# An attention and gated feed-forward kernel on one core: token chunks of 512, one per batch, in place of chunks of 384

## Chip, cores and metric

The kernel runs on one NeuronCore of a Trainium2 chip. The metric is device microseconds (us) of one execution of the whole program; the median of several runs is compared. Five engines work side by side, each through its own instructions in program order: TensorE (PE, matmuls; PEld is its weight load, which runs beside the matmuls), VectorE (DVE), ScalarE (ACT), GpSimd (POOL) and SyncE (SP, which here only issues DMA transfers).

## What is computed

Eight batches of 576 tokens, eight heads of 64. Heads 0 to 3 attend to a local window of 32 tokens, heads 4 to 7 to the tokens whose position has the same remainder by 32. The 4608 x 512 result goes through a feed-forward layer with a gate.

```python
batch, n_heads, seq, head_dim = (8, 8, 576, 64)
mask_local = (rel >= 0) & (rel < stride)            # stride = 32
mask_strided = (rel >= 0) & (pos[None, :] % stride == pos[:, None] % stride)
...
attn = attn / (np.sum(attn, axis=-1, keepdims=True) + 1e-09)
...
# n_tokens, d_model, d_ff = (4608, 512, 2048)
h = x @ w_in
sp = np.maximum(h, 0.0) + np.log1p(np.exp(-np.abs(h)))
g = h * erf(sp)
return (g @ w_out).astype(np.float32)
```

## The kernel before

**Feed-forward.** The tokens are cut into twelve chunks of `CH` = 384 (line 20), three for each pair of batches: the first lies in the even batch, the second takes the last 192 tokens of the even and the first 192 of the odd batch, the third lies in the odd batch. For each chunk and each of the sixteen 128-column slices f of the hidden layer, `ftile` (line 665) does one set of work. `mm1` (line 674, its matmul is line 678) makes h as 12 matmuls of 384 columns: every fp32 operand is held as a high and a low fp32r part (`xhi`, `xlo` and the pair of each weight), and three of the four products are taken for each of four slices of the model dimension. Then ten steps on ACT and DVE turn h into the gated g and split it: `n1` (ACT, reads the PSUM bank of h), `n2` (DVE), `n3`, `n4` (ACT), `n5`, `n6` (DVE), `n7`, `gate` (ACT), `prod` (DVE, writes the product back into the bank of h), `split_hi` (ACT, line 716) and `split_lo` (DVE, line 719). ACT's functions are recorded at line 686, DVE's three-operand steps at line 683. `mm2` (line 747, matmul at line 750) is nine matmuls of 512 columns, three for each of the three 128-token tiles, added up in three output banks `o0` to `o2` over the slices f. After the last f of a segment ACT copies each output bank to `ob` (`evac`, line 766) and SP stores it (line 769); later segments of the same chunk are added in DRAM by a DMA that POOL issues (line 772).

**Order of the first chunks.** While the weights come in, the first three chunks are worked in turns, four slices at a time: `SEGS` (line 84) has nine segments, (0,0,4), (1,0,4), (2,0,4), (0,4,8) and so on, the last three being slices 8 to 16. From chunk 3 on, a chunk runs through all sixteen slices. `weight` (line 610) loads each of 32 weight slices as 64-bit numbers and makes fp32 and then the pair of it: three bit operations and a subtraction on DVE, a cast on ACT (lines 628 to 649).

**Attention.** `heads` (line 324) does one unit of two heads, 4 units a batch, 32 in all: q, k and v are loaded by SP (lines 378 and 386), 80 or 48 small matmuls make scores (line 400), maximum, difference, exponential and sum follow on DVE and ACT, POOL divides (`norm`, line 498), PE transposes (line 507), ACT copies the result to a tile `pt` (line 513), 72 or 44 small matmuls make x (line 526), and ACT and DVE split x into `xhi` and `xlo` (lines 545 and 550). These two hold a ring of two batches of tokens. A unit of batch b writes its part of the ring after the chunks that read the batch two before it have been through `mm1`.

**What sets the order.** `Plan` (line 158) writes out one fixed order for each engine ahead of time, from keys (`FT`, `KW`, `KP`, `SLOT`) and a model of durations; the engines then run that order and wait on semaphores. `bufs` (line 301) gives the number of buffers of each kind: 3 banks for h, 2 buffers each for `a`, `b`, `ghi`, `glo`, `sm` and `pt`, and one bank each for `o0` to `o2`. Two more PSUM banks belong to attention. `TWO` (line 144) names the DVE steps that the plan keeps apart from POOL's work. Until the first feed-forward work PE fills gaps with matmuls on constants (`warm`, line 858).

```python
            terms = [(w, x, cc) for w, x in ((0, xhi), (1, xhi), (0, xlo)) for cc in range(NCC)]
            for i, (w, x, cc) in enumerate(terms):
                yield nc.tensor.matmul(
                    ph[:, :CH], win[4 * s + cc][:, w, fs], x[cc][:, c0 : c0 + CH], start=(i == 0), stop=(i == len(terms) - 1)
                )
```

Of the kernel before, what the change touches and what calls it, by code (L numbers as in the profile page):

```python
# [19 lines left out]
CH = 384  # L20
NCHUNK = NT // CH
# [8 lines left out]
SLOT = 4.6  # L30
BACKLOG = 1.1130116
FT = (31.6335, -135.614, 224.291, 52.3709, -149.741, 22.9733, 45.4447, 151.185, -55.3448, 2.76331, -71.5147, 15.0393)
KI = 6.0
KW = (
# [4 lines left out]
)  # L39
KP = (  # L40
    (10.1977, 20.0763, 41.7156, 4.63147, -42.1192, -1.63969, 44.6351),
    (-59.6923, -46.4572, 19.3027, 2.1291, -1.1102, -2.7047, 19.8359),
    (0.362135, -29.4861, 70.4804, -32.303, -26.5488, -31.8946, 13.368),
    (35.4136, 29.0365, 82.2259, 1.42982, 5.30056, -34.5623, 14.0121),
    (39.729, -4.01849, 28.501, 2.48999, 23.3488, 1.39481, -48.8561),
    (39.4267, -19.5662, -38.0465, 15.7041, 15.7802, 2.62076, 21.1909),
    (86.1182, 25.9137, 40.603, 35.2787, 19.0606, 47.8996, 48.8007),
    (66.293, 47.5794, 1.05774, -1.16663, 5.84633, 49.4365, 8.65975),
    (130.703, 144.013, 104.668, 48.8468, 193.869, 96.8577, 143.58),
    (64.6189, 239.715, 128.496, 148.929, 218.31, 111.72, 213.914),  # L50
    (83.8361, 207.928, 161.012, 201.508, 232.12, 168.377, 236.359),
    (122.833, 130.354, 229.613, 323.83, 280.389, 244.736, 254.984),
    (275.847, 231.102, 232.486, 247.903, 285.925, 244.698, 249.036),
    (249.04, 261.206, 282.841, 273.283, 271.781, 286.07, 316.395),
    (257.063, 302.313, 270.687, 300.842, 280.135, 302.865, -52.5488),
    (271.303, -41.686, 283.568, 283.624, 288.229, 313.902, -30.1178),
# [908 lines left out]
```

## Time and profile before

| | |
|---|---|
| three runs | 931.13, 931.49, 933.93 us; median 931.49 us |
| profiled execution, its own time | 933.05 us |
| its span, first to last instruction | 931.3 us |
| busy: PE, PEld | 909.7 us (98%), 809.6 us (87%) |
| busy: DVE, ACT, POOL | 686.7 us (74%), 653.4 us (70%), 60.9 us (7%) |
| mean granted TensorE clock | 0.993 of full |

A share of busy time is a mean over stages with different limits. The stages here are: until 43.7 us attention of the first batches and loads, without feed-forward work; until about 200 us feed-forward while weights are still being made; until about 733 us feed-forward with attention of later batches between; until 917.9 us feed-forward alone; then the end. A matmul's duration in a row holds its way through the array and overlaps the next one's, so what a matmul costs is read from the distance between starts.

### The profile page before, as it was taken

To read this page: it belongs to the slowest core of one execution; us is meant where nothing else is said; L and a number is where in the kernel's file an instruction comes from. 1 tells how busy PE (TensorE), PEld (TensorE's weight loads), DVE (VectorE), ACT (ScalarE), POOL (GpSimd) and SP (SyncE) were. 2 spreads that over 40 slices of the span, in tenths; PEclk is the share of its full clock that TensorE was granted. 3 is DMA by queue.
4 is the path that set the end of the run, shared out by engine and by line. 5 is a ranking of instruction groups with operands and counts; after the bars stand their busy time and mean duration, and the time that the engine had idled before them with its cause. 6 is when DMAs were issued, how large, how long until landed. Compare 5 with 4: busy or idle time off the path is not lost.

```text
span 931.3 us, 20134 instructions
## 1 busy us (share of the span) xinstructions
PE 909.7 (98%) x8166; PEld 809.6 (87%) x8169; DVE 686.7 (74%) x1352; ACT 653.4 (70%) x1476; POOL 60.9 (7%) x59
## 2 busy tenths in 40 slices
PE   5789999999999999999999999999999999999998
PEld 4678888898888889988888899998898899999997
DVE  5999999996757766669886876667876666666664
ACT  5687887887776767667666666766766766766765
POOL 2200012110101100001110100000100000000000
PEclk9799999999999999999999999999999999999999
DMA  9994124321313010013312300002300200000000
GB/s 336 391 362 154 62 57 73 61 34 48 78 58 86 30 64 35 27 57 105 99 56 92 124 17 1 34 1 73 135 1 30 70 1 1 34 1 0 34 1 35
DMA packets 23421, 68.86 MB, mean 74 GB/s; under 512 B 2592, under 2 KB 3232, under 8 KB 23328
## 3 DMA queue, kind: packets, MB, share of 16 engines
q1 hardware_dynamic: 20736, 62.86, 18.9%
q0 software_dynamic: 2592, 4.72, 3.6%
q8 instruction: 64, 1.05, 0.5%
q14 instruction: 29, 0.24, 0.1%
HBM read 53.41 MB, written 14.16 MB: 73 GB/s over the span
## 4 chain that ended last, share of the span: by engine, by line
PE 90%; DVE 4%; ACT 3%; issue 1%; DMA 1%; SPq 0%; POOL 0%; ACTq 0%; POOLq 0%
PE h L678 41%; PE o L750 40%; PE s L400 3%; PE x L526 3%; PE t L507 2%; PE s L526 1%; DMA qk<-qk_loc 1%; ACT b L686 1%; DVE a L683 1%; DVE b L683 1%; ACT a L686 1%; PE s L507 1%; DVE glo L719 1%; ACT sm L472 0%; DVE h L713 0%
## 5 line engine op out<-in xcount | busy, mean ns | idle before, releaser
L750 PE MATMUL o<-pair,ghi 128*128 128x512 f32 x1152 | 361.4, 395 | 0.2 <-ACT ghi L716 0.2
L678 PE MATMUL h<-xhi,pair 128*128 128x384 f32 x1536 | 302.4, 339 | 0.6 <-DVE glo L719 0.6
L678 PEld LDWEIGHTS h<-xhi,pair 128*128 128x128 f32 x1536 | 271.4, 188 | 16.5 <-DVE glo L719 2.6
L686 ACT ACTIVATE b<-b 128x384 f32<-128x384 f32 x384 | 200.4, 522 | 77.2 <-DVE b L683 73.8
L750 PEld LDWEIGHTS o<-pair,ghi 128*128 128x128 f32 x1152 | 209.8, 188 | 32.4 <-ACT ghi L716 0.7
L750 PE MATMUL o<-pair,glo 128*128 128x512 f32 x576 | 224.8, 390 | 0.0
L683 DVE SCALAR_TENSOR_TENSOR a<-h,a 128x384 f32<-128x384 f32 x192 | 106.3, 553 | 83.3 <-ACT a L686 82.8
L678 PE MATMUL h<-xlo,pair 128*128 128x384 f32 x768 | 164.4, 336 | 0.0
L686 ACT ACTIVATE a<-h 128x384 f32<-128x384 f32 x192 | 93.5, 487 | 100.9 <-PE h L678 100.2
L683 DVE SCALAR_TENSOR_TENSOR a<-a,h 128x384 f32<-128x384 f32 x192 | 105.5, 549 | 68.9 <-ACT b L686 68.9
L713 DVE TENSOR_TENSOR h<-b,h 128x384 f32<-128x384 f32 x192 | 107.0, 557 | 46.2 <-ACT b L686 45.8
L678 PEld LDWEIGHTS h<-xlo,pair 128*128 128x128 f32 x768 | 136.0, 188 | 0.0
L750 PEld LDWEIGHTS o<-pair,glo 128*128 128x128 f32 x576 | 108.1, 188 | 23.7 <-DVE glo L719 0.3
L686 ACT ACTIVATE a<-a 128x384 f32<-128x384 f32 x192 | 100.3, 523 | 26.6 <-DVE a L683 26.1
L719 DVE TENSOR_TENSOR glo<-h,ghi 128x384 fp32r<-128x384 f32 x192 | 105.7, 550 | 11.7 <-ACT ghi L716 10.2
L716 ACT CAST ghi<-h 128x384 fp32r<-128x384 f32 x192 | 90.5, 471 | 29.1 <-DVE h L713 15.1
L683 DVE SCALAR_TENSOR_TENSOR b<-b,a 128x384 f32<-128x384 f32 x192 | 108.7, 566 | 1.0
L686 ACT ACTIVATE b<-a 128x384 f32<-128x384 f32 x192 | 101.0, 526 | 4.4
L498 POOL TENSOR_TENSOR sm<-sm,r 128x768 f32<-128x768 f32 (+3 forms) x36 | 45.0, 1249 | 435.3 <-DVE r L491 330.9
L436 DVE TENSOR_REDUCE mx<-s 128x12 f32<-128x768 f32 (+3 forms) x37 | 28.8, 784 | 10.6 <-PE s L413 10.3
L766 ACT COPY ob<-o 128x512 f32<-128x512 f32 x54 | 31.0, 588 | 2.7 <-PE o L750 2.2
L526 PEld LDWEIGHTS x<-pt,v 64*64 64x64 f32 x1392 | 24.4, 135 | 6.9 <-issue 4.4
(49 smaller groups left out, 511.4 us busy)
## 6 DMA issues: line engine op xcount, KB each, us to landing
out<-ob SPq DMA_DIRECT2D x36, 256.0 KB, 2.0
v<-v_loc SPq DMA_DIRECT2D x13, 640.0 KB, 4.1
words<-w_in SPq DMA_DIRECT2D x16, 512.0 KB, 8.6
words<-w_out SPq DMA_DIRECT2D x16, 512.0 KB, 9.1
qk<-qk_loc SPq DMA_DIRECT2D x13, 592.0 KB, 3.8
qk<-qk_str SPq DMA_DIRECT2D x12, 608.0 KB, 3.8
v<-v_str SPq DMA_DIRECT2D x16, 384.0 KB, 3.3
out<-ob POOLq DMA_DIRECT2D x18, 256.0 KB, 4.6
```

The lines of the kernel that those rows point to most:

```text
L436: yield nc.vector.tensor_reduce(out=mx[:, parts[i], :units], in_=wide(of(s, i)), axis=mybir.AxisListType.X, op=ALU.max)
L498: yield (nc.gpsimd if pool_norm else nc.vector).tensor_tensor(out=d, in0=d, in1=spread(rc, i), op=ALU.mult)
L507: yield nc.tensor.transpose(bank(t, h)[:, 128 * w : 128 * w + 128], sm[:, h, c : c + 128], ident)
L526: yield nc.tensor.matmul(bank(px, m)[h * D : (h + 1) * D, a * n : (a + 1) * n], values(rows, (2 * a + h) * D), pt[rows, h, c : c + n], sta ...
L678: yield nc.tensor.matmul(ph[:, :CH], win[4 * s + cc][:, w, fs], x[cc][:, c0 : c0 + CH], start=(i == 0), stop=(i == len(terms) - 1))
L683: yield nc.vector.scalar_tensor_tensor(out=out, in0=in0, scalar=scalar, in1=in1, op0=op0, op1=op1)
L686: yield nc.scalar.activation(dst, src, func, bias=bias[i], scale=scale)
L713: yield nc.vector.tensor_tensor(out=ph[:, :CH], in0=bb.tile, in1=ph[:, :CH], op=ALU.mult)
L716: yield nc.scalar.copy(ghi.tile, ph[:, :CH])
L719: yield nc.vector.tensor_tensor(out=glo.tile, in0=ph[:, :CH], in1=ghi.tile.bitcast(F32), op=ALU.subtract)
L750: yield nc.tensor.matmul(po.tile, g[:, ts], wout[f][:, w], start=(f == first_f and i == 0), stop=(f == last_f and i == 2),)
L766: yield nc.scalar.copy(ob.tile, po.tile)
```

## The change

Chunks have 512 tokens: chunk b is the first 512 tokens of batch b. The last 64 tokens of each batch, in `xhi` and `xlo`, are written by SP to a tensor `rests` in DRAM as soon as a unit of attention has made them (64 transfers of 128 rows of 256 bytes); after batch 7 and after chunk 6 has been through its `mm1`, POOL issues eight loads that bring them back, and they make chunk 8. So there are nine chunks and 144 sets in place of twelve and 192. `mm1` has 12 matmuls of 512 columns, `mm2` 12 for four token tiles and four output banks `o0` to `o3`; h has two PSUM banks in place of three. A new step `keep` on ACT copies h from PSUM to an SBUF tile `hs` (three buffers); `n5`, `prod`, `split_hi` and `split_lo` then read `hs` and not the bank, and `prod` writes into `hs`. `n6`, `n7` and `gate` work in `a`, so that `b` is free after `n6`; `b` has one buffer. `SEGS` has six segments of the first two chunks. `pt` shares the buffer of `sm`. Chunk 8's rows are stored by two transfers a tile. The keys of the order are other numbers throughout.

```diff
-CH = 384
-NCHUNK = NT // CH
+CH = 512
+REST = S - CH
...
-SLOT = 4.6
+SLOT = 6.1
...
-    (("h", "o2"), (23, 8, 9, 10), True, True),
+    (("o2", "o3"), (23, 8, 9, 10), True, True),
...
-    (None, (14, 15, 28), False, False),
-    (("o1", "o2"), (29, 30, 31), True, True),
+    (("o2", "o3"), (14, 15, 28), True, True),
+    (None, (29, 30, 31), False, True),
...
-SEGS = ((0, 0, 4), (1, 0, 4), (2, 0, 4), (0, 4, 8), (1, 4, 8), (2, 4, 8), (0, 8, 16), (1, 8, 16), (2, 8, 16))
+SEGS = ((0, 0, 4), (1, 0, 4), (0, 4, 8), (1, 4, 8), (0, 8, 16), (1, 8, 16))
...
-TWO = {"n6", "norm", "bits0", "bits1", "bits2", "split_lo_w"}
+TWO = {"n5", "n6", "prod", "split_lo", "norm", "bits0", "bits1", "bits2", "split_lo_w"}
...
-    ps_h = ctx.enter_context(tc.tile_pool(name="ps_h", bufs=3, space=PSUM))
+    ps_h = ctx.enter_context(tc.tile_pool(name="ps_h", bufs=2, space=PSUM))
...
-    bufs = {"qk": 1, "v": 1, "sm": 2, "pt": 2, "mx": 2, "r": 2, "ps": 1, "h": 3, "a": 2, "b": 2, "ghi": 2, "glo": 2,
+    bufs = {"qk": 1, "v": 1, "sm": 2, "mx": 2, "r": 2, "ps": 1, "h": 2, "hs": 3, "a": 2, "b": 1, "ghi": 2, "glo": 2,
...
+            pt = sm if home is None else pt
...
+        hs = buf("mpool", "hs", [P, CH], f"hs_{k}")
...
-            c0, fs, s = (c % 3) * CH, slice(f * P % SW, f * P % SW + P), f * P // SW
+            c0, fs, s = c % 2 * S, slice(f * P % SW, f * P % SW + P), f * P // SW
...
+        def keep():
+            yield nc.scalar.copy(hs.tile, ph.tile)
...
-            yield from stt(a.tile, a.tile, C5, ph[:, :CH], ALU.mult, ALU.add)
+            yield from stt(a.tile, a.tile, C5, hs.tile, ALU.mult, ALU.add)
...
-            yield from stt(bb.tile, bb.tile, C6, a.tile, ALU.add, ALU.mult)
+            yield from stt(a.tile, bb.tile, C6, a.tile, ALU.add, ALU.mult)
...
-            yield nc.vector.tensor_tensor(out=ph[:, :CH], in0=bb.tile, in1=ph[:, :CH], op=ALU.mult)
+            yield nc.vector.tensor_tensor(out=hs.tile, in0=a.tile, in1=hs.tile, op=ALU.mult)
...
-            yield nc.scalar.copy(ghi.tile, ph[:, :CH])
+            yield nc.scalar.copy(ghi.tile, hs.tile)
...
-            yield nc.vector.tensor_tensor(out=glo.tile, in0=ph[:, :CH], in1=ghi.tile.bitcast(F32), op=ALU.subtract)
+            yield nc.vector.tensor_tensor(out=glo.tile, in0=hs.tile, in1=ghi.tile.bitcast(F32), op=ALU.subtract)
...
+        o_c = add("act", tp, at(12), keep, [first], [hs], [ph])
...
-        o = add("dve", td, at(4), n5, [o], [], [a, ph])
+        o = add("dve", td, at(4), n5, [o, o_c], [], [a, hs])
...
-                    yield nc.sync.dma_start(out[c * CH + t * P : c * CH + (t + 1) * P, :], ob.tile)
+                    if c < B:
+                        yield nc.sync.dma_start(out[c * S + t * P : c * S + (t + 1) * P, :], ob.tile)
+                        return
+                    for n in range(2):
+                        r = (2 * t + n) * S + CH
+                        yield nc.sync.dma_start(out[r : r + REST, :], ob[n * REST : (n + 1) * REST, :])
...
+    def stash(b, hp, part, x, done):
+        def run():
+            c0 = b % 2 * S + CH
+            yield nc.sync.dma_start(rests[hp, part, :, b * REST : (b + 1) * REST], x[hp][:, c0 : c0 + REST].bitcast(F32))
+
+        return plan.add("sp", 0.1, KP[4 * b + hp][6] + (1.0 + 0.1 * part), run, done)
+
+    def reload(hp, part, x, after):
+        def run():
+            yield nc.gpsimd.dma_start(out=x[hp][:, :CH], in_=rests[hp, part].bitcast(F32R))
...
-                c = 3 * (p2 - 1) + b % 2
-                done, _, _, _ = heads(b, hp, keys, [mm1_of[c], mm1_of[c + 1]], last_av)
...
+                done, _, _, _ = heads(b, hp, keys, [mm1_of[b - 2], *put[b - 2]], last_av)
+            x_of.setdefault(b, []).extend(done)
+            put.setdefault(b, []).extend(stash(b, hp, n, x, done) for n, x in enumerate((xhi, xlo)))
...
+        if b == B - 1:
+            free = [mm1_of[B - 2], *(o for n in put for o in put[n])]
+            x_of[B] = [reload(hp, n, x, free) for hp in range(NCC) for n, x in enumerate((xhi, xlo))]
+            chunk(B, 0, NFC)
```

## Rows read from the trace of the kernel before

**Rows 1.** The profile page: the span, part 1 (busy us, share of the span, instructions), the granted TensorE clock in 40 slices of the span, and part 4, the chain that ended last, by engine.

```profile
span 931.3 us, 20134 instructions
...
PE 909.7 (98%) x8166; PEld 809.6 (87%) x8169; DVE 686.7 (74%) x1352; ACT 653.4 (70%) x1476; POOL 60.9 (7%) x59
...
PEclk9799999999999999999999999999999999999999
...
PE 90%; DVE 4%; ACT 3%; issue 1%; DMA 1%; SPq 0%; POOL 0%; ACTq 0%; POOLq 0%
```

**Rows 2.** Busy time in stretches. Columns: stretch, its length, busy us (and instructions) of PE, PEld, DVE, ACT and POOL, granted clock, mean share of the DMA engines, GB/s.

```profile
0.00:43.70 43.70, 29.32 (x781) 22.05 (x783) 31.19 (x75) 26.51 (x113) 10.12 (x15) 0.86 0.98 361
43.70:66.70 23.00, 20.59 (x338) 16.93 (x337) 22.27 (x51) 17.50 (x55) 1.94 (x2) 0.97 0.99 394
46.00:186.00 140.00, 136.96 (x1165) 120.67 (x1165) 136.81 (x278) 112.89 (x259) 13.92 (x14) 1.00 0.43 130
186.00:890.00 704.00, 703.64 (x6033) 631.90 (x6032) 494.79 (x954) 488.09 (x1050) 36.85 (x30) 1.00 0.15 47
```

**Rows 3.** The chain that ended last, in order of time, in the stage of feed-forward work alone. Columns: start us, us, engine, tile, line, matmuls. Fifteen sets lie between the first and the last row.

```profile
747.61 2.09 PE h L678 x12
749.69 2.04 PE o L750 x9
...
809.51 2.09 PE h L678 x12
```

**Rows 4.** Part 5 of the page: groups of matmuls by line and shape (count, busy us, mean ns of one, idle before them).

```profile
L750 PE MATMUL o<-pair,ghi 128*128 128x512 f32 x1152 | 361.4, 395 | 0.2 <-ACT ghi L716 0.2
L678 PE MATMUL h<-xhi,pair 128*128 128x384 f32 x1536 | 302.4, 339 | 0.6 <-DVE glo L719 0.6
```

**Rows 5.** Groups by line with shapes kept apart, ACT first, then DVE: out<-in, shape, count, busy us, mean ns of one, idle us before them and who ended it. `a<-h` on ACT is n1, `a<-a` n3, `b<-a` n4, `b<-b` n7 and gate; on DVE `a<-h,a` is n2, `a<-a,h` n5, `b<-b,a` n6.

```profile
L686 ACT ACTIVATE b<-b 128x384 f32<-128x384 f32 x384 | 200.4, 522 | 77.2 <-DVE b L683 73.8
L686 ACT ACTIVATE b<-a 128x384 f32<-128x384 f32 x192 | 101.0, 526 | 4.4
L686 ACT ACTIVATE a<-a 128x384 f32<-128x384 f32 x192 | 100.3, 523 | 26.6 <-DVE a L683 26.1
L686 ACT ACTIVATE a<-h 128x384 f32<-128x384 f32 x192 | 93.5, 487 | 100.9 <-PE h L678 100.2
L716 ACT CAST ghi<-h 128x384 fp32r<-128x384 f32 x192 | 90.5, 471 | 29.1 <-DVE h L713 15.1 <-PE o L750 13.3 <-PE h L678 0.3
L766 ACT COPY ob<-o 128x512 f32<-128x512 f32 x54 | 31.0, 588 | 2.7 <-PE o L750 2.2 <-DMA out<-ob 0.3
L646 ACT CAST pair<-w 128x512 fp32r<-128x512 f32 x32 | 20.1, 627 | 2.2 <-DVE w L641 1.9
...
L683 DVE SCALAR_TENSOR_TENSOR b<-b,a 128x384 f32<-128x384 f32 x192 | 108.7, 566 | 1.0
L713 DVE TENSOR_TENSOR h<-b,h 128x384 f32<-128x384 f32 x192 | 107.0, 557 | 46.2 <-ACT b L686 45.8
L683 DVE SCALAR_TENSOR_TENSOR a<-h,a 128x384 f32<-128x384 f32 x192 | 106.3, 553 | 83.3 <-ACT a L686 82.8
L719 DVE TENSOR_TENSOR glo<-h,ghi 128x384 fp32r<-128x384 f32 x192 | 105.7, 550 | 11.7 <-ACT ghi L716 10.2
L683 DVE SCALAR_TENSOR_TENSOR a<-a,h 128x384 f32<-128x384 f32 x192 | 105.5, 549 | 68.9 <-ACT b L686 68.9
L649 DVE TENSOR_TENSOR pair<-w,pair 128x512 fp32r<-128x512 f32 x32 | 22.8, 712 | 0.9 <-ACT pair L646 0.9
```

**Rows 6.** The end of the program in order of time: start us, us, engine, line, operation, count, and in brackets the idle time before it and who ended it.

```profile
918.03 0.86 PE L678 MATMUL h<-xlo,pair 128*128 128x384 f32 x4
...
919.21 0.47 ACT L686 ACTIVATE a<-h 128x384 f32<-128x384 f32 x1
...
924.62 0.39 PE L750 MATMUL o<-pair,glo 128*128 128x512 f32 x1
924.71 0.48 ACT L716 CAST ghi<-h 128x384 fp32r<-128x384 f32 x1 [0.68 <-DVE h L713]
...
925.24 0.73 PE L750 MATMUL o<-pair,ghi 128*128 128x512 f32 x2 [0.23 <-ACT ghi L716]
...
926.98 1.70 SPq L769 DMA_DIRECT2D out<-ob  x3
```

**Rows 7.** POOL beside DVE: one of POOL's divisions and the DVE subtraction that starts beside it, in order of time; then all of POOL's divisions (part 5 of the page), and, of the tile `pair`, the durations of the DVE subtraction (min/median/max ns, first and last start).

```profile
38.14 1.26 POOL L498 TENSOR_TENSOR sm<-sm,r 128x640 f32<-128x640 f32 x1 [0.44 <-ACT qk L513]
...
38.19 1.75 DVE L649 TENSOR_TENSOR pair<-w,pair 128x512 fp32r<-128x512 f32 x1
...
L498 POOL TENSOR_TENSOR sm<-sm,r 128x768 f32<-128x768 f32 (+3 forms) x36 | 45.0, 1249 | 435.3 <-DVE r L491 330.9
...
L649 DVE TENSOR_TENSOR pair<-w,pair x32: 628/681/1755, 15.3 to 199.6; 128x512 fp32r<-128x512 f32 x32
```

**Rows 8.** DMA issues: engine, count, size, median us from issue to landing; and SP's own waits by line (us in total, times, longest): line 386 is the load of v.

```profile
out<-ob SPq DMA_DIRECT2D x36, 256.0 KB, 2.0
...
SPq L386 <- PE x L526: 273.3, 22, 51.7
```

More of the change, by code (lines that the diff above doesn't have):

```diff
@@ L586, in heads @@
             y = t[i] if len(t) > 1 else t[0]
-            o = add("pe", 0.33 * (p.stop - p.start) + 0.05, k_t + e, turn(i), [o, o_ident] + first[2:3], ([pt] if i == 0 and home is None else []) + ([y] if not own else []), [sm, y])
+            o = add("pe", 0.33 * (p.stop - p.start) + 0.05, k_t + e, turn(i), [o, o_ident] + first[2:3], [y] if not own else [], [sm, y])
             first.append(o)
@@ L688, in n1 @@
         def n1():
-            yield from fun(a.tile, ph[:, :CH], AF.Tanh, 0, S1)
+            yield from fun(a.tile, ph.tile, AF.Tanh, 0, S1)
+        def keep():
+            yield nc.scalar.copy(hs.tile, ph.tile)
         def n2():
-            yield from stt(a.tile, ph[:, :CH], C2, a.tile, ALU.mult, ALU.add)
+            yield from stt(a.tile, ph.tile, C2, a.tile, ALU.mult, ALU.add)
         def n3():
@@ L725, in at @@
             return FT[i] + v0
-        first = add("pe", 2.09, v0, mm1, ready[0] + mm1_first[-1:], [ph])
+        first = add("pe", 2.73, v0, mm1, ready[0] + mm1_first[-1:], [ph])
         first.words = 24
         o = add("act", tp, at(0), n1, [first], [a], [ph])
+        o_c = add("act", tp, at(12), keep, [first], [hs], [ph])
         o = add("dve", td, at(1), n2, [o], [], [ph, a])
@@ L732, in ftile @@
         o = add("act", ta, at(3), n4, [o], [bb], [a])
-        o = add("dve", td, at(4), n5, [o], [], [a, ph])
+        o = add("dve", td, at(4), n5, [o, o_c], [], [a, hs])
         o = add("dve", td, at(5), n6, [o], [], [a, bb])
-        o = add("act", ta, at(6), n7, [o], [], [bb])
-        o = add("act", ta, at(7), gate, [o], [], [bb])
-        o = add("dve", td, at(8), prod, [o], [], [bb, ph])
-        o_h = add("act", tp, at(9), split_hi, [o] + hi_of[-1:], [ghi], [ph])
+        o = add("act", ta, at(6), n7, [o], [], [a])
+        o = add("act", ta, at(7), gate, [o], [], [a])
+        o = add("dve", td, at(8), prod, [o], [], [a, hs])
+        o_h = add("act", tp, at(9), split_hi, [o] + hi_of[-1:], [ghi], [hs])
         hi_of.append(o_h)
-        o_l = add("dve", td, at(10), split_lo, [o_h], [glo], [ph, ghi])
+        o_l = add("dve", td, at(10), split_lo, [o_h], [glo], [hs, ghi])
         last = []
@@ L802, in attention_moe @@
     o_ps, order_o, stored = [None] * NTT, [None] * NTT, {}
-    x_of, w_load, turns = {}, [], {}
+    x_of, put, w_load, turns = {}, {}, [], {}
+    rests = nc.dram_tensor("rests", (NCC, 2, P, B * REST), F32, kind="Internal").ap()
     mm1_of, mm1_first, hi_of = {}, [], []
@@ L827, in chunk @@
             mm1_of[c] = o
-    def chunks_of(b, hp, m):
-        if hp < 2 and m == b % 2:
-            return [0] if b % 2 == 0 else [2]
-        return [0, 1] if b % 2 == 0 else [1, 2]
+    def stash(b, hp, part, x, done):
[6 more added lines that the diff above has]
+            yield nc.gpsimd.dma_start(out=x[hp][:, :CH], in_=rests[hp, part].bitcast(F32R))
+        o = plan.add("pool", 1.2, PRO + SLOT * (len(mm1_first) - 8) + hp + 0.1 * part, run, after)
+        o.tail = 2.5
+        return o
     last_av = []
@@ L865, in warm @@
         return w, run
-    w, run = warm("o2")
+    w, run = warm("o3")
     first = plan.add("pe", 0.217, -10.0, run, o_con, [w])
-    plan.filler = (first, warm, ("o2", "o1", "o0", "ps"), mm1_first[6])
+    plan.filler = (first, warm, ("o3", "o2", "o1", "o0", "ps"), mm1_first[6])
     for op in plan.order():
```

88 lines of the change are left out of this document (42 added, 46 removed), and 8 rows, old and new, of the table KW.

## The prediction

> **What bounds the kernel now.** I read the profile page first. PE is busy 98% of the span, the granted clock is at its upper level (2.4 GHz) in all but the first slices, and PE makes up 90% of the chain that ended last [rows 1]. Then the stretches [rows 2]: from 186 to 890 us PE idles 0.36 us in 704, while DVE and ACT are busy 70% and 69%. So in that stage only PE's own work counts. What is lost lies in front, where PE idles 14.4 us before 43.7 and 2.4 us in the next 23 us, and at the end, where the last matmuls wait for `ghi` and a copy and a store follow them [rows 6]. A second limit shows between 46 and 186 us: DVE is busy 136.81 of 140 us there, beside a PE that is busy 136.96 [rows 2]. That stage makes the weights.
>
> Since PE is the limit, its price for one matmul is what matters. In the stage of feed-forward work alone the chain is nothing but `mm1` and `mm2` in turns. Fifteen sets take 809.51 - 747.61 = 61.90 us, 4.1267 us each [rows 3]; the fifteen `mm1` among them (the first is the 2.09 of the rows) sum to 31.25 us, 2.083 us for 12 matmuls, and the nine of `mm2` take the other 2.043. That is 173.6 ns for 384 columns and 227.0 ns for 512. The groups' means, 339 and 395 ns [rows 4], hold the way through the array and are no price. Two widths give two unknowns: 53.4 ns for 128 columns, which is 0.417 ns for one (2.4 GHz), and a fixed 13.4 ns for each matmul whatever its width. The rounding of the rows leaves about 1 ns either way on the fixed part.
>
> **The change, part by part.**
>
> *Wider matmuls.* The columns stay the same: 192 x (12 x 384 + 9 x 512) = 144 x 24 x 512 = 1,769,472. The matmuls fall from 192 x 21 = 4032 to 144 x 24 = 3456, by 576. Before: 192 x 4.127 = 792.3 us. After: a set is 24 x 0.2270 = 5.448 us, 144 of them 784.5 us. The difference is -7.8 us (576 x 13.4 ns = 7.7), or -7.1 to -8.3 us by the two ends of the fixed part. All of it lies on the path, since PE sets the end.
>
> The Trainium skill (TensorE: Matmul & The Clock Gate, section Back-to-back issue gap) gives a gap of N/2.4 + 2.5 ns at the full clock. By its fixed part the saving would be 576 x 2.5 ns = 1.4 us, by the rows it is 7.8 us; the trace does not agree with the page here, as 512 columns take 227.0 ns and not 215.8.
>
> *More work on ACT, none of it in front of PE by itself.* An op of 384 columns takes 487 (n1), 526, 523, 522 (twice) and 471 ns [rows 5]. The two copies out of PSUM differ by 588 - 471 = 117 ns for 128 columns, so I take +117 each: n1 604, `n3`, `n4`, `n7` and `gate` 640 each, `keep` 588 as the copy of that shape, `split_hi` 627 as the cast of a weight from SBUF. That is 4.38 us a set and 631 us in all, for 586 now (200.4 + 101.0 + 100.3 + 93.5 + 90.5): ACT goes from 653 to some 698 us, 75% of the span, and is the limit nowhere on average. It costs nothing as long as PE's other sets cover it; in the stage from 46 to 186 us it goes from 113 to some 120 of 140 us.
>
> *Less work on DVE.* Five ops a set of 549 to 566 ns become five of about 690 (the subtraction of 512 columns takes 712 with its median at 681 [rows 5, 7]): 3.45 us a set, 497 us for 533. That relieves the stage where DVE is full by about 4 us.
>
> *The chain behind each h.* Now the last one runs from the end of `mm1` (918.03 + 4 x 0.174 = 918.73) to `ghi` at 925.19, 6.5 us, with PE occupied almost to the end by 27 matmuls of older sets [rows 6]: it idles 0.23 us. With six ACT ops at +0.117 and four DVE ops at +0.14 the chain takes 7.7 us, and up to 8.3 with `keep` in its way. In mid-run, if `mm2` follows two sets behind its `mm1`, two further `mm1` and two older `mm2` lie between (4 x 2.72 = 10.9 us), so the chain stays hidden with 2.6 us to spare. Two banks of h are enough: a bank is free after `n1`, `keep` and `n2`, some 2 us behind its `mm1`, where now it is held to `split_lo`. `a` is held from `n1` to `prod` (some 7 us of the 10.9 that two buffers give), the single `b` from `n4` to `n6` (some 2.5 of 5.4). Costed at nothing; without the cover each 0.1 us a set is 14 us.
>
> *The end.* There the chain's growth shows: 7.7 to 8.3 us against two older sets (24 x 0.227 = 5.4 us) or three (8.2), so 0 to 2.9 us of idle time for 0.23 now. Two stores a tile in place of one add about 0.3 us. I take +1.3 us, between 0 and +3.
>
> *The start.* Four segments of 8 sets give 43.6 us of PE work per four slices of weights for both chunks, where 12 sets give 49.5 now. The second group of weights is so wanted 5.9 us sooner after the first `mm1`, the third 11.8 us sooner; the last weight is wanted at the same time (24 x 5.448 = 130.8 for 32 x 4.127 = 132.1). DVE, being 98% busy there, can't make up all of it. Against it stand the 4 us that DVE saves, and four `mm1` of 2.72 us (two banks freed early, then two more) ahead of the first `mm2` where three of 2.08 fit now, 4.6 us more cover in the stretch in which PE idles 2.4 us. Bounds -4.6 and +11.8 us; neither end has a nearer row than the other, and I take 0.
>
> *DMA.* The 64 stashes (32 KB each) go on SP, behind the split of each unit; queued behind a waiting one are the next loads of q, k, v and the stores. SP spends 273 us waiting with the load of v alone [rows 8], so its time costs nothing, unless a load lands late for a PE whose order is fixed: 0 to some 2 us, taken as 0. The DMA engines are 15% occupied from 186 to 890 us [rows 2]. The eight reloads on POOL have the whole of chunk 7 (16 x 5.448 = 87 us) to land, and nothing but each other behind them. `pt` in the buffer of `sm`, 52 evacuations for 54, and the moves of attention cost PE nothing: its small matmuls are the same, and 70% of DVE leaves room.
>
> Sum: -7.8 + 1.3 + 0 = -6.5 us. The profiled execution takes 933.05 us, 1.75 over its span of 931.3; it would take 926.5. It lies 1.56 us above the median of the runs, 931.49, so the median goes to **925.0 us** (-0.7%).
>
> **The rivals.**
>
> *The fixed part belongs to the columns.* If 512 columns in `mm1` cost 4/3 of 173.6 ns, a set takes 2.78 + 2.72 = 5.50 us, and 144 take 792: no gain, and with the end 932.8 us. For it: `mm1` has other operands than `mm2`. Against it: two widths on one line of 0.417 ns, exactly the granted clock. Chance 0.04, and the time is the same.
>
> *Weights come late.* DVE's order between 46 and 186 us is the bound, and PE waits at the second and third group. Price up to 11.8 us, so 931.5 - 7.8 + 1.3 + 11.8 = 936.8. From 3.7 us of waiting on the time is within the same, from 9.3 on it is slower. For it: DVE at 98%. Against it: DVE's own work falls, its idle time before 43.7 us is 12.5 us [rows 2], and the last deadline doesn't move. Chances: 0.09 the same, 0.08 slower.
>
> *POOL holds DVE.* Four of five DVE steps now read two SBUF tiles, where only `n6` did. When POOL divides, such a step stretches: 1.75 us for 0.68, beside a division of 1.26 us [rows 7]. Some 26 of the 36 divisions come after the start, 1.25 us each: at worst 32 us. The spare 2.6 us of the chain takes one at a time, so I expect nothing of it; if a third came through, -6.5 + 10.8 gives 935.8 us. Chance 0.03: 0.02 the same, 0.01 slower. The Trainium skill (SBUF — State Buffer, section SBUF: two separate sides) names an exclusive port pair that a DVE op with two SBUF inputs and a GpSimd op that reads SBUF can't hold together; the stretched row agrees.
>
> *The start gains.* If early weights use DVE's idle time and the longer cover fills PE, -4.6 us or a little more: 918 to 920.5 us. Chance 0.10.
>
> **How the numbers follow.** The forecast, with its own range of 920.5 to 928.7, has 0.66, the rivals 0.04, 0.17, 0.03 and 0.10. A difference of 0.3% (2.8 us) is about what a measurement of this kernel tells from none. Faster: 0.66 + 0.10 = 0.76; same: 0.04 + 0.09 + 0.02 = 0.15; slower 0.09. The range from 917.5 takes in the start's gain, up to 931.5 half of the cases in which weights are late.
>
> **What would show it.** In the stage of feed-forward alone, a set every 5.45 us, twelve starts in 2.72 us for `mm1` as for `mm2`; that carries the sum. PE idle below 1 us between 190 and 890; more, behind ACT or DVE, and the chain is not covered. Idle PE between 44 and 190 us behind `pair` shows late weights, a stretched DVE step beside POOL the port, idle time before the last twelve matmuls the end. The prediction is wrong if `mm1` takes more than 2.75 us, or if PE idles over 20 us in front of its first 190 us.

## The result: slower by 0.7% where 0.7% faster was forecast

The changed kernel takes 938.12 us (median of four runs, 937.79 to 939.09), the kernel before beside it 931.62 (931.13 to 933.93): a ratio of 1.0067 with a 95% interval of 1.0048 to 1.0085. The profiled execution spans 936.0 us for 931.3 before.

The page of the changed kernel, the lines that answer to [rows 1]:

```profile
span 936.0 us, 18645 instructions
...
PE 909.9 (97%) x7589; PEld 728.6 (78%) x7593; DVE 680.5 (73%) x1111; ACT 687.7 (73%) x1330; POOL 69.7 (7%) x66
```

It has 576 matmuls fewer (7593 for 8169, counted by weight loads), and PE is busy as long as before, 909.9 for 909.7 us. So the matmuls that are left got dearer. The stretches of [rows 2], in the changed kernel, at the upper level of the clock from 43.7 us on:

```profile
0.00:43.70 43.70, 29.64 (x739) 20.11 (x743) 35.40 (x80) 24.91 (x106) 9.16 (x14) 0.92 0.93 336
43.70:66.70 23.00, 18.97 (x371) 14.64 (x373) 22.58 (x47) 21.35 (x67) 5.25 (x5) 1.00 0.96 344
46.00:186.00 140.00, 136.67 (x1080) 109.36 (x1072) 133.66 (x237) 120.93 (x246) 12.09 (x13) 1.00 0.43 132
186.00:890.00 704.00, 703.32 (x5578) 566.77 (x5577) 488.55 (x760) 513.99 (x928) 46.88 (x39) 1.00 0.18 54
```

PE idles 0.68 us between 186 and 890 us, where it idled 0.36 before. The chain behind h, the weights, DVE and POOL therefore cost nothing there that shows as idle time. The price lies in the distance between the matmuls, and the chain shows it (start us, us, engine, tile, line, matmuls; compare [rows 3]):

```profile
804.77 2.80 PE h L679 x12
807.57 2.75 PE o L755 x12
810.32 2.80 PE h L679 x12
```

A set takes 810.32 - 804.77 = 5.55 us, forecast 5.448. `mm1` takes 2.80 for 2.72. From start to start in the records its matmuls lie 232 and 235 ns apart in turn, 233.3 in the mean: 512 / 2.4 + 20.0 ns, where `mm1` of 384 columns took 384 / 2.4 + 13.3 and the `mm2` of before 512 / 2.4 + 13.3 (2.4 columns per ns is the upper level of the clock). `mm2` pays too: its first five gaps are 230, 236, 228, 233 and 231 ns, the rest 226.7.

Where the whole span went, by adding up for every matmul the time to the start of the next (us; the third column is an experiment below):

| | before | changed | changed, x moved by 32 bytes |
|---|---|---|---|
| up to the first matmul | 5.6 | 5.0 | 5.0 |
| `mm1` | 407.2 | 407.7 | 398.2 |
| `mm2` | 403.5 | 406.7 | 405.3 |
| attention and warm-up matmuls | 111.0 | 109.4 | 112.7 |
| from the last matmul's start to the end | 4.0 | 7.1 | 7.1 |
| span | 931.3 | 936.0 | 928.3 |

Two things stand out: the feed-forward matmuls take 3.7 us more instead of 7.8 less, and the end is 3.1 us longer instead of 1.3. The columns are one profiled execution each. The row of attention holds waits too and differs between executions of like work (113.3 us in the profile of the fourth output buffer below, for 109.4 here), so its differences are not read as effects. The end of the changed kernel (start us, us, engine, line, operation, count; answers to [rows 6]):

```profile
927.30 1.95 ACT L771 COPY ob<-o 128x512 f32<-128x512 f32 x3 [3.00 <-PE o L755]
...
927.91 5.20 SPq L779 DMA_DIRECT2D out<-ob  x8
...
931.14 0.58 ACT L771 COPY ob<-o 128x512 f32<-128x512 f32 x1 [1.89 <-DMA out<-ob]
```

Eight stores, one behind the other every 0.65 us, take SP's queue 5.20 us, and the fourth copy waits 1.89 us for one of three output buffers. Each of these stores of 64 rows holds the queue 0.47 to 0.59 us, where a store of 128 rows, as in the other chunks, holds it 0.33 us.

### The profile page after: what moved, and what is told of

It reads as the page before. It is cut to its first block, busy times and chain, and to the rows that moved or that the text cites. A ratio compares the mean times of both kernels' runs of the same rounds, so it can differ in the third digit from the quotient of the medians.

```text
span 936.0 us, 18645 instructions
## 1 busy us (share of the span) xinstructions
PE 909.9 (97%) x7589; PEld 728.6 (78%) x7593; DVE 680.5 (73%) x1111; ACT 687.7 (73%) x1330; POOL 69.7 (7%) x66
## 4 chain that ended last, share of the span: by engine, by line
PE 83%; issue 5%; DVE 5%; DMA 4%; ACT 2%; SPq 0%; POOL 0%; ACTq 0%; POOLq 0%; DVEq 0%
PE o L755 38%; PE h L679 38%; PE x L526 3%; PE s L400 2%; DMA qk<-qk_str 2%; PE t L507 1%; DVE a L684 1%; ACT a L687 1%; DMA words<-w_in 1%; DMA out<-ob 1%; DVE glo L723 1%; DMA v<-v_str 0%; DVE hs L717 0%; DVE mx L436 0%; PE s L526 0%
## 5 line engine op out<-in xcount | busy, mean ns | idle before, releaser
L687 ACT ACTIVATE a<-a 128x512 f32<-128x512 f32 x432 | 262.8, 631 | 52.5 <-DVE a L684 51.2
L679 PE MATMUL h<-xhi,pair 128*128 128x512 f32 x1152 | 294.2, 397 | 0.2 <-DVE a L684 0.2
L679 PE MATMUL h<-xlo,pair 128*128 128x512 f32 x576 | 157.6, 395 | 0.0
L723 DVE TENSOR_TENSOR glo<-hs,ghi 128x512 fp32r<-128x512 f32 x144 | 102.6, 713 | 71.6 <-ACT ghi L720 71.3
L717 DVE TENSOR_TENSOR hs<-a,hs 128x512 f32<-128x512 f32 x144 | 105.7, 734 | 63.5 <-ACT a L687 63.5
L684 DVE SCALAR_TENSOR_TENSOR a<-a,hs 128x512 f32<-128x512 f32 x144 | 99.4, 690 | 47.0 <-ACT hs L693 33.1
L684 DVE SCALAR_TENSOR_TENSOR a<-h,a 128x512 f32<-128x512 f32 x144 | 98.8, 686 | 31.9 <-ACT a L687 16.9
L720 ACT CAST ghi<-hs 128x512 fp32r<-128x512 f32 x144 | 88.4, 614 | 22.2 <-PE o L755 20.8
L684 DVE SCALAR_TENSOR_TENSOR a<-b,a 128x512 f32<-128x512 f32 x144 | 100.5, 698 | 2.1
L687 ACT ACTIVATE b<-a 128x512 f32<-128x512 f32 x144 | 89.9, 624 | 0.4
```

Source lines behind the costliest of these rows:

```text
L679: yield nc.tensor.matmul(ph[:, :CH], win[4 * s + cc][:, w, fs], x[cc][:, c0 : c0 + CH], start=(i == 0), stop=(i == len(terms) - 1))
L684: yield nc.vector.scalar_tensor_tensor(out=out, in0=in0, scalar=scalar, in1=in1, op0=op0, op1=op1)
L687: yield nc.scalar.activation(dst, src, func, bias=bias[i], scale=scale)
L717: yield nc.vector.tensor_tensor(out=hs.tile, in0=a.tile, in1=hs.tile, op=ALU.mult)
L720: yield nc.scalar.copy(ghi.tile, hs.tile)
L723: yield nc.vector.tensor_tensor(out=glo.tile, in0=hs.tile, in1=ghi.tile.bitcast(F32), op=ALU.subtract)
```

## The experiments

The question was why 512 columns cost 20 ns over N/2.4 in `mm1` and 13.3 in the `mm2` of before. The two have other operands: in `mm1` the weights are the stationary operand and x the moving one, in `mm2` g is stationary and weights move. By the order and the sizes in which the pools hand out the tiles, the weight pairs and `ghi`/`glo` all start at one place modulo 256 bytes, and the tiles of x 32 bytes (8 columns of 4 bytes) below it. No trace shows an address; the runs of matmuls alone, below, set the starts by hand and give the same prices. Both kernels are alike in this. My theory was that this place counts. The rivals were the width alone, the order in which the operands follow each other, the start flag and the bank, and the work that the changed kernel does beside PE.

**Widths, order and place, one chunk each.** In the changed kernel, chunk 2 stays as it is. Chunks 7 and 8 read x 8 and 16 columns further on, so they multiply other tokens; chunks 4 to 6 leave out columns.

```diff
+            if c == 3:
+                terms = [(w, x, cc) for cc in range(NCC) for w, x in ((0, xhi), (1, xhi), (0, xlo))]
+            wide = {4: 384, 5: 480, 6: 504}.get(c, CH)
+            c0 += {7: 8, 8: 16}.get(c, 0)
             for i, (w, x, cc) in enumerate(terms):
+                n = CH if i == 0 else wide
...
```

> The changed kernel with mm1 altered from chunk to chunk, so one trace holds several prices of a matmul; mm2 and everything else as in the changed kernel, where mm1 takes 233.4 ns a matmul. Chunk 2: unaltered. Chunk 3: the three products of one slice of the model dimension behind each other, so that two matmuls in a row read the same moving columns. Chunks 4, 5 and 6: after the first matmul only 384, 480 and 504 columns are multiplied, so the last columns of h lack eleven of twelve terms. Chunks 7 and 8: the moving columns start 8 and 16 columns (32 and 64 bytes) further on, so other tokens are multiplied. Theory W (width: the extra 6.7 ns comes when a matmul fills the whole PSUM bank): 384, 480 and 504 columns cost N/2.4 + 13.3 ns, that is 173.3, 213.3 and 223.3, and the order and the start don't matter. Theory S (a steady state of the stream in which each matmul of more than some width runs late): 384 at 173.3, 480 and 504 already above N/2.4 + 13.3 by some ns. Theory O (operands: what lies behind each other, or where it starts, makes the extra): chunk 3, 7 or 8 falls to 226.7 ns at the full width.

The chain, rows from the chunks with 384 and 480 columns (the first of the twelve is 512 wide), +8 columns (with the `mm2` behind it) and +16:

```profile
516.73 2.16 PE h L684 x12
...
573.56 2.65 PE h L684 x12
...
813.25 2.72 PE h L684 x12
815.97 2.72 PE o L760 x12
...
829.69 2.80 PE h L684 x12
```

Eight columns further on, `mm1` falls to 2.72 us and the `mm2` behind it is flat; sixteen columns on, it is back at 2.80. The same instruction with the same width costs 226.7 or 233.3 ns by where its moving operand starts. The order (chunk 3) changes nothing: 233.3 for 233.2. 480 and 504 columns cost 219.5 and 229.7 ns, 6 ns more than N/2.4 + 13.3; 384 columns settle at 173. So theory W, a price of the full bank, falls; theory S holds for the widths and theory O for the start.

**Other operands.** In the changed kernel again, with other operands in five chunks (h there is no longer the layer's), with every matmul starting a new sum in chunk 7, and with six `mm2` in one bank in chunk 8.

```diff
+                lhs, rhs = win[4 * s + cc][:, w, fs], x[cc][:, c0 : c0 + CH]
+                if c == 2:
+                    rhs = x[0][:, c0 : c0 + CH]
+                if c == 3:
+                    lhs = win[4 * s][:, 0, fs]
+                if c == 4:
+                    rhs = win[4 * s + cc][:, w]
+                if c == 5:
+                    lhs = x[cc][:, c0 + 128 * (f % 4) : c0 + 128 * (f % 4) + 128]
+                if c == 6:
+                    lhs, rhs = x[cc][:, c0 + 128 * (f % 4) : c0 + 128 * (f % 4) + 128], win[4 * s + cc][:, w]
-                    ph[:, :CH], win[4 * s + cc][:, w, fs], x[cc][:, c0 : c0 + CH], start=(i == 0), stop=(i == len(terms) - 1)
+                    ph[:, :CH], lhs, rhs, start=(i == 0 or c == 7), stop=(i == len(terms) - 1 or c == 7)
...
+                if c == 8 and first_f < f < last_f and t == 1:
+                    po = o_ps[0]
```

> The changed kernel with the operands of mm1 altered from chunk to chunk; h is wrong in them, the counts and shapes of instructions are the same. Chunk 2: all twelve matmuls read the moving columns of the first slice of the model dimension (xhi or xlo). Chunk 3: all twelve load the same stationary columns. Chunk 4: the moving columns come from the weight pair (512 columns of it). Chunk 5: the stationary columns come from xhi and xlo. Chunk 6: both, the operands with their places changed. Chunk 7: every matmul starts a new sum in the bank in place of adding to it. Chunk 8: the matmuls of mm2 for the second token tile are added into the first tile's bank, so six in a row write one bank and not three (the second tile keeps only its first and last slice). Theory O (place of the operands): chunk 4 or 5 or 6 falls from 233.4 to 226.7 ns. Theory P (adding twelve times into one bank of 512 columns makes the extra): chunk 7 falls to 226.7 ns, and in chunk 8 the six in a row of mm2 show more than 226.7. Theory L (twelve different stationary loads): chunk 3 falls. Under a state of the stream that has nothing to do with operands all stay at 233.4.

The chain, one `mm1` of chunk 4 and one of chunk 6:

```profile
518.28 2.72 PE h L690 x12
...
706.24 2.80 PE h L690 x12
```

With both operands from weight tiles (chunk 4) a matmul takes 227.5 ns, with both from x (chunk 5) 228.5, with the two swapped (chunk 6) 233.2. One tile for all twelve, moving or stationary, changes nothing (233.2), nor does the start flag (233.3); the six `mm2` in one bank run as those in three, with the same first five gaps and 226.7 after. So it is the places of the two operands together, not one operand and not where results go.

**The wide `mm1` in the kernel before.** There chunks 9, 10 and 11 get 512, 448 and 496 columns (columns behind the chunk's own are read along and not used; chunk 11 starts 112 columns earlier, so as to fit the ring).

```diff
+            wide = {9: 512, 10: 448, 11: 496}.get(c, CH)
+            c0 = min(c0, RING - wide)
...
```

> The kernel before with mm1 widened in its last chunks: chunk 9 multiplies 512 columns, chunk 10 448, chunk 11 496, of which the first 384 are used (moving columns begin where they still fit the ring, so some tokens are the wrong ones). Its mm1 takes 173.3 ns for 384 columns. If the extra belongs to 512 columns in mm1 whatever the layout, chunk 9 shows 233.4 ns; if it belongs to the layout, the order or the ACT and DVE work of the changed kernel, chunk 9 shows 226.7. 448 and 496 columns: 200.0 and 220.0 ns under a full-bank theory, some ns more if the extra grows with the width.

```profile
792.82 2.06 PE o L752 x9
794.89 2.80 PE h L680 x12
...
808.83 2.45 PE h L680 x12
```

512 columns take 2.80 us there too, and 448 take 2.45, 203.6 ns each for 448 / 2.4 + 13.3 = 200.0; the 496, at a start of their own, take 224.4 for 220.0. So it is none of the changed kernel's banks, copies or ACT work.

**A fourth output buffer** for the last chunk (the tile of v, which is free by then):

```diff
-                ob = buf("mpool", "ob", [P, DM], f"ob{t}_{k}")
+                if c == B and t == 3:
+                    ob = buf("apool", "v", [P, WV], f"ob{t}_{k}")
+                else:
+                    ob = buf("mpool", "ob", [P, DM], f"ob{t}_{k}")
...
```

> The changed kernel with one alteration: in chunk 8 the copy of the fourth token tile goes to the buffer of v, which attention no longer needs, and not to the first of the three ob buffers. In the trace of the changed kernel the last copy starts at 931.14 us, 1.89 us after ACT was free, held by the store that empties its buffer. Theory (three buffers for four tiles delay the end): the copy follows the third at about 929.4 us, the span shrinks by 1.5 to 1.9 us, 936.4 us for 938.1. Rival (the stores, eight in a row on SP, set the end anyway): less than 0.5 us.

It took 938.99 us (938.14 to 943.64), 1.0062 [1.0035, 1.0089] of the kernel before: as the changed kernel. Its four copies ran in one go, 2.63 us, and from the last matmul's start to the end it still took 7.1 us. So the wait for the buffer had cost nothing, as the rival said: the eight stores last longer anyway.

**x moved by 32 bytes.** The first version that should undo the loss. `con_e`, one column that takes 32 bytes of the pool, is allocated ahead of x instead of behind it; not one instruction differs, only where x lies.

```diff
+    con_e = cpool.tile([P, 1], F32, name="con_e")
     xhi = [cpool.tile([P, RING], F32R, name=f"xhi{c}") for c in range(NCC)]
     ...
-    con_e = cpool.tile([P, 1], F32, name="con_e")
```

> The changed kernel with one edit: the 32-byte tile con_e is allocated ahead of the tiles of x instead of behind them, so that x lies 32 bytes higher and starts at the same place modulo 64 bytes as the weight pairs; nothing else moves and no instruction changes. Theory (the price is the differing place of the moving and the stationary operand of a wide matmul): mm1 falls from 233.3 to 226.7 ns a matmul and mm2 loses its unsettled first matmuls, a set of 24 from 5.547 to 5.44 us, 144 sets x 0.107 = 15.4 us less, some 922.5 us; faster than the kernel before by 0.9%, about what was forecast of the change itself. Rival (the +8 columns of the earlier run helped through which values or rows were read, or the gain is eaten by another engine that becomes late): no change of mm1, 938, or mm1 at 226.7 and gaps elsewhere, over 930.

929.19 us (927.0 to 933.73), 0.9963 [0.995, 0.9976] of the kernel before (933.36 there): 1% less than the changed kernel's 1.0067. Its chain:

```profile
804.59 2.72 PE h L679 x12
807.31 2.72 PE o L755 x12
```

A set is 5.44 us, the forecast's 5.448, and the gaps are 226 and 227 ns. The saving over the changed kernel in `mm1` and `mm2` is 10.9 us (table above), not the 15.4 expected. That sum took the clean sets for all 144. Over the run, what gaps above 260 ns in `mm1` and `mm2` hold over the clean price sums to 17.8 us, for 16.1 in the changed kernel and 15.9 before; the other gaps average 227.2 in `mm1` and 227.7 in `mm2`. What makes these gaps grow by 1.7 us was not tried.

**The same move in the kernel before.**

> The kernel before with the same move of con_e, so that its x too starts at the same place as the weight pairs. Its mm1 is 384 wide and costs N/2.4 + 13.3 ns already (173.3). Theory: the narrow matmul hides the price of the place, so no change, within 0.3% of the kernel before, 931 to 933. Rival (the place costs narrow matmuls too, and the attention's): faster by over 0.3%.

940.59 us, 1.008 [1.0066, 1.0094] of the kernel before (933.36): slower, against both theories. `mm1` of 384 columns and the `mm2` behind it, at equal places now (for 2.09 and 2.04 us in [rows 3]):

```profile
794.98 2.10 PE h L678 x12
797.08 2.08 PE o L750 x9
```

The gaps of `mm1` begin 171, 175, 177, 185, 176, 182 and settle at 173; those of `mm2` are 229, 233, 236, 224, 231, 236, 228, 233 and do not settle within nine. So equal places are good for 512 beside 512 and bad for 384 beside 512. My theory in the form "equal places cost least" fell here.

**Other places** in the changed kernel (other columns of x in chunks 2 to 8, and fewer columns in chunks 6 to 8):

```diff
+            c0 += {2: 4, 3: 12, 4: 24, 5: 32, 6: 8, 7: 8, 8: 8}.get(c, 0)
+            wide = {6: 384, 7: 448, 8: 480}.get(c, CH)
...
```

> The changed kernel with the moving operand of mm1 shifted, by chunk: chunk 2 by 4 columns (16 bytes), chunk 3 by 12 (48), chunk 4 by 24 (96), chunk 5 by 32 (128), chunks 6, 7 and 8 by 8 columns (32 bytes) at 384, 448 and 480 columns (values are then not the reference's). Theory (the two operands' places modulo 64 bytes): 24 columns cost 226.7 as 8 do, 32 cost 233.3 as none does; widths 384, 448 and 480 at 8 columns cost N/2.4 + 13.3: 173.3, 200.0 and 213.3, where unshifted 448 took 203.6 and 480 took 219.5. 4 and 12 columns are open: 226.7 if anything but equality modulo 64 to the unshifted place helps, 233.3 if only a start 32 bytes off does. Rival (a period other than 64 bytes, or a matter of the ring's end): chunk 4 at 233.3 or chunk 5 at 226.7.

The chain, a set of chunk 4 (+24 columns):

```profile
520.59 2.77 PE o L758 x12
523.36 2.76 PE h L682 x12
```

The means were 233.7 (+4), 231.2 (+12), 229.6 (+24), 234.0 (+32), and at +8 columns 175.8 for 384, 202.7 for 448 and 216.8 for 480. The theory wanted 226.7 at +24 and N/2.4 + 13.3 at the three widths, and missed all four; only its 233.3 at +32 came (234.0). The place counts, but not as a matter of equal or unequal.

**Matmuls alone.** A kernel with nothing but float32r matmuls of 128 stationary columns, 48 in a row for each setting (n moving columns from column m, stationary columns from column w, two tiles 4096 bytes apart), and then blocks of 12 in turns. In short:

```
for i in range(48):
    nc.tensor.matmul(p[:, :n], wb[:, w : w + 128], xb[:, m : m + n], start=(i == 0), stop=(i == 47))
```

> A kernel of matmuls alone, which computes nothing of the reference: float32r matmuls with 128 stationary columns from one tile and n moving columns from another that lies 4096 bytes higher, 48 in a row for each setting of the width n, of the moving start m and of the stationary start w (in columns of 4 bytes); then blocks of 12 with n = 512 or 384 in turn with blocks of 12 with 512 columns, at starts of their own. Theory 1 (equality of the two places modulo 64 bytes decides): n/2.4 + 13.3 ns wherever m - w is 0, 16, 32, 64, some n/2.4 + 20 where it is 8 or 24 and n is 448 or more, 384 at 173.3 everywhere, and blocks of 384 at equal places followed by 512 at equal places flat. The kernel before with x shifted speaks against it: 384 at equal places took 175.8 and the 512 behind it 231. Theory 2 (the place and the width act together: what counts is where in SBUF the moving stream stands when the weight load runs beside it, so that a width that is 128 columns less turns the good place into a bad one): the good m - w of 384 and of 512 differ, and within one width the price goes up and down with m. Theory 3 (only the change between two kinds of matmul costs): all 48 in a row are flat at n/2.4 + 13.3 after the first few, and the price stands in the blocks in turn alone.

The chain, in which the tile's name is the setting (n, m, w) and each row is 48 matmuls:

```profile
26.67 10.88 PE n512m0w0s L312 x48
37.55 11.12 PE n512m4w0s L312 x48
48.67 11.20 PE n512m8w0s L312 x48
...
71.07 11.00 PE n512m16w0s L312 x48
...
204.78 10.92 PE n512m64w0s L312 x48
...
248.67 10.89 PE n512m0w4s L312 x48
...
326.43 11.04 PE n512m4w4s L312 x48
...
426.00 8.33 PE n384m0w0s L312 x48
...
495.71 9.90 PE n448m8w0s L312 x48
...
515.36 9.60 PE n448m16w0s L312 x48
```

Divided by 48, 512 columns cost, at w = 0, 226.7 ns at m = 0, 231.7 at 4, 233.3 at 8, 229.2 at 16, and are back near 226.7 at 64. For 448 columns at w = 0 the best start of those tried is 16 (200.0) and 8 the worst (206.3). Equal starts are no rule here either: at m = w = 4 the 512 columns cost 230.0. So the price goes up and down with the start, and each width has a pattern of its own: theory 2 of the expectation holds in what it says of prices. The blocks in turns, with the four kernels' settings (`a` is `mm1`, `b` is `mm2`, whose starts are 8 and 8):

```profile
1096.04 2.80 PE n512m0w8v88a L312 x12
1098.84 2.75 PE n512m0w8v88b L312 x12
...
1183.94 2.72 PE n512m8w8v88a L312 x12
1186.66 2.72 PE n512m8w8v88b L312 x12
...
1418.43 2.08 PE n384m0w8v88a L312 x12
1420.51 2.72 PE n384m0w8v88b L312 x12
...
1495.74 2.10 PE n384m8w8v88a L312 x12
1497.85 2.76 PE n384m8w8v88b L312 x12
```

From top to bottom these are the changed kernel (2.80 and 2.75), the one with x moved (2.72 and 2.72), the kernel before (2.08, and 2.72 for twelve is its 2.04 for nine) and the kernel before with x moved (2.10; 2.76 for its 2.08 for nine). Matmuls with no other engine at work give all four prices, so width, the two starts and the stream that ran before are enough to explain them. Theory 3 (only the change between two kinds costs) falls for the changed kernel, whose 233.3 ns 48 in a row pay too. In the kernel before with x moved it is the change that costs: in a row, 384 and 512 columns at starts 8 and 8 settle at 173.3 and 226.7.

**Stationary columns, bfloat16, period, narrow widths.** The same kind of kernel:

> Matmuls alone again, 48 in a row for each setting, nothing of the reference: (a) 512 moving columns with 128, 96, 64 and 32 stationary columns at four pairs of starts; (b) both operands bfloat16; (c) moving starts from 68 to 128 columns, and 192, 320 and 384; (d) widths from 128 to 464 at starts 0/0 and 0/8. Theory 1 (the fixed part is the load of the next stationary columns, which holds up the moving columns read beside it): the 13.3 ns over n/2.4 fall with the stationary columns, to some 10, 6.7 and 3.3 at 96, 64 and 32, the spread between starts falls with them, and bfloat16 halves both. Theory 2 (the fixed part is the matmul's own, whatever it loads): 13.3 at every number of stationary columns. For (c): the price of a start repeats after 64 columns (256 bytes) if 60, 64, 128 and 256 columns at 226.7 in the earlier run are its period, so 192, 320 and 384 are at 226.7. For (d): the price grows with the width in steps and not evenly, as 480 and 496 already did.

```profile
26.85 10.88 PE n512m0w0k128r L317 x48
...
115.55 11.05 PE n512m0w0k64r L317 x48
...
159.75 11.11 PE n512m0w0k32r L317 x48
...
246.05 7.80 PE n384m0w0k128h L317 x48
253.85 7.80 PE n384m16w0k128h L317 x48
...
455.40 10.88 PE n512m192w0k128r L317 x48
...
488.04 5.31 PE n128m0w0k128r L317 x48
```

(a) Fewer stationary columns (k) do not make the fixed part smaller, 11.05 us with 64 and 11.11 with 32 for 10.88 with 128: my theory 1, a price per stationary column, falls. (b) With both operands bfloat16 (`h`) the price is 7.80 / 48 = 162.5 ns for 384 columns, 384/2.4 + 2.5, at all four pairs of starts tried. The larger fixed part and the dependence on the start were seen with float32r only. (c) 192, 320 and 384 columns on, the price is 226.7 again, and starts of 68 to 128 columns repeat the prices of 4 to 64: a period of 64 columns (256 bytes), as far as was tried. (d) At 128 and 192 columns, the two widths tried below 256, a float32r matmul costs 111 to 112 ns (5.31 / 48 = 110.6 for 128), so there the width no longer sets the price.

**The shorter end, first try**: the aligned kernel, the fourth buffer, and one store for each of the last four tiles, whose two halves belong to two batches:

```diff
-                    for n in range(2):
-                        r = (2 * t + n) * S + CH
-                        yield nc.sync.dma_start(out[r : r + REST, :], ob[n * REST : (n + 1) * REST, :])
+                    rest = out.rearrange("(b s) d -> b s d", s=S)[2 * t : 2 * t + 2, CH:, :]
+                    yield nc.sync.dma_start(rest, ob[:, :DM])
```

> The aligned kernel of this call, and a fourth output buffer for the last chunk together with one store for each of its four tiles instead of two (the two batches of a tile in one transfer). Theory of the end (eight stores of 0.65 us each on SP's queue set the 6.7 us behind the last matmul): the stores take 4 x 0.65 = 2.6 us less 5.2, so the end is 4.1 us and the time 2.0 to 2.6 us under the aligned kernel, some 920 us. Rival (the last transfer's landing sets the end, or a store of two pieces takes twice as long): no change beside the aligned kernel.

945.07 us, 1.0128 [1.011, 1.0146]. It is slower than the aligned kernel by 16 us, against both theories. PE was done no later (last matmul's start 919.51, there 921.16), and then 23 us passed:

```profile
918.51 9.64 SPq L781 DMA_DIRECT2D out<-ob  x4
```

The four transfers, 1.05 MB together, flowed at some 51 GB/s with the DMA engines 12% occupied, the work of about two of sixteen. The slowest dimension of the destination has size 2 now. By the Trainium skill (DMA: Bandwidth & Descriptors, section on why a DMA increments its semaphore by 16 and not by 1) the size of the slowest dimension bounds the number of engines that share a transfer; the trace agrees.

**The shorter end, second try**: the eight plain stores again, half of them issued by ACT.

```diff
+                def store_b(t=t, ob=ob):
+                    r = (2 * t + 1) * S + CH
+                    yield nc.scalar.dma_start(out[r : r + REST, :], ob[REST:, :DM])
...
+                    if c == B:
+                        add("act", 0.06, o.key + 0.1, store_b, [o], [], [ob])
```

> The aligned kernel (x moved by 32 bytes) with a fourth output buffer for the last chunk, and the last chunk's eight stores of 64 rows shared between two queues: the first half of each tile from SP, the second half from ACT, as eight plain transfers. Theory of the end (the eight stores of 0.65 us in a row on one queue set the 6.7 us behind the last matmul, and the transfers themselves are short): four on each side end 2.6 us sooner, the end falls to some 3.6 to 4.2 us, the time 2.5 to 3.5 us under the aligned kernel, 925.5 to 927, about 0.993 of the kernel before. Rival (ACT's copies wait on its own stores, or the landing of the last transfer sets the end): 0 to 1 us gained, 928 to 929.

929.24 us, 0.9968 [0.9954, 0.9982]: no different from the aligned kernel.

```profile
922.39 4.12 SPq L781 DMA_DIRECT2D out<-ob  x4
...
925.43 0.59 ACT L774 COPY ob<-o 128x512 f32<-128x512 f32 x1 [0.57 <-ACT ob L774]
926.05 0.50 ACTq L785 DMA_DIRECT2D out<-ob  x1
```

ACT's own stores, 0.5 us each, stand between its copies, and SP's four stores wait for the copies. From the last matmul's start (923.39) to the end it takes 6.5 us for 7.1. The rival was right here, and no run brought the end back to 4.0 us.

## Why the prediction was wrong

**The step that failed** is the first of the sum: "a fixed 13.4 ns for each matmul whatever its width". Two widths give two unknowns only if nothing else differs between them, and the two came from different operands. That they fell on one line with the granted clock was taken as proof, and the rival that named the operands got 0.04. In fact both pairs stood on good settings, 384 columns at starts 0 and 8 and 512 at 8 and 8 (blocks in turns above), and the change made the first pair 512 wide, where its starts are bad: 233.3 ns, and some 24 ns more for the `mm2` behind it (2.745 for 2.72 us). A clean set is 5.547 us for 5.448, which over 144 sets is 14 us against a forecast gain of 7.8. The prediction's own sign, `mm1` over 2.75 us, came. Over the whole run `mm1` and `mm2` missed by 11.5 us (+3.7 for -7.8) and not by 14, since the kernel before does not keep its clean prices either: its gaps below 260 ns average 174.3 and 227.7, for 173.6 and 227.0.

**The mechanism of the gain was right**, on operands that stand well. With x moved by 32 bytes a set takes 5.44 us, and `mm1` and `mm2` over the whole run take 7.2 us less than before (803.5 for 810.7), forecast 7.8. The change lost this gain to the places of two tiles, which no line of its diff shows.

**The rival nearest in mechanism, "the fixed part belongs to the columns",** gave 932.8 us and was wrong in its reason: 512 columns did not cost 4/3 of 384 (231.5 ns) but 233.3, and by their place. Its argument, that `mm1` has other operands than `mm2`, was the right one. The two rivals nearer in time, late weights (936.8) and POOL (935.8), did not occur.

**ACT and the chain behind h** went as forecast: ACT is busy 687.7 us (forecast 698), and PE's idle time from 186 to 890 us rose by 0.32 us. **DVE** was relieved less than forecast: its five steps sum to 507 us (forecast 497, before 533), and `prod` takes 734 ns for some 690. Its busy time between 46 and 186 us fell by 3.2 us, forecast about 4. Neither cost PE anything that shows.

**The end** was mis-sized: +3.1 us for +1.3, of a range of 0 to +3, and from another cause. The chain to the last `ghi` cost nothing; the eight stores did, priced at 0.3 us without a row. SP's queue is done with them 4.2 us after the last matmul's start, for 1.4 us before, which is 2.8 of the 3.1 us. That is read from the chain: the one run that shortened the queue gained 0.6 us.

**The start and the late weights**: PE idles 14.1 and 4.0 us in the first two stretches, for 14.4 and 2.4 before, and 3.33 for 3.04 us between 46 and 186. In the first 190 us together that is 18.7 for 17.4, so the 0 that I took was 1.3 us off. That is less than two profiles of like work differ: with the fourth output buffer, PE idles 16.5 us in the first stretch.

**POOL beside DVE and the stashes** cost nothing that the trace shows in PE's idle time.

What stays open is the cause inside the chip. The runs show the price as a function of width, starts, type and what ran before, not which memory or queue holds up which stream. The difference of the starts alone is no rule either: equal starts of 0 cost 226.7 and equal starts of 4 cost 230.0 ns, and +4 columns in the changed kernel (starts 4 and 8) cost 233.7, while matmuls alone at starts 0 and 4 cost 226.9 (10.89 us for 48).

## What to carry to other kernels

When a change alters only the width of a float32r matmul, price the new width on the operands that it will have: a kernel of matmuls alone, with the real widths, the real starts modulo 256 bytes and the real neighbours in turn, gives in one run what two rows of the old profile can't. If PE sets the end and a matmul costs more than its neighbour of the same width, move a tile by 32 bytes before anything else; here that was worth 1% and cost nothing, and the same move made the other kernel 0.8% slower. At the end of a program count the stores that one queue issues, and keep a large dimension outermost in each (an outermost 2 cost 16 us here).

## What the runs showed of the hardware that was not expected

- A float32r matmul of 512 columns costs 226.7 to 234.6 ns by the starts of its two operands (48 in a row). Behind an `mm1` at other starts, `mm2` takes five matmuls to come back to 226.7, and behind 384 columns at equal starts it doesn't within nine.
- For bfloat16 the fixed part is 2.5 ns at every start tried. That is the fixed part of the gap that the Trainium skill (TensorE: Matmul & The Clock Gate, section Back-to-back issue gap) gives for a matmul on its own; the bfloat16 rows, 48 in a row, agree with it and the float32r rows don't.
- A store of 64 rows holds the queue that issues it for some 0.55 us on SP (every 0.65 us, one behind the other) and 0.5 us on ACT, where it stands between ACT's own operations; a store of 128 rows holds SP for 0.33 us. Why fewer rows take longer was not tried.
